# Eight filter transfers placed behind a step of the angle tables, with w_phi's transfers ahead of them

## The chip, the cores and the metric

The kernel runs on one core of one Trainium2 chip. The metric is device time in microseconds of one execution. A run's time is a little longer than the span of the profile, which goes from the first to the last profiled instruction.

The names of the engines in the profile: PE is TensorE (matmuls; PEld its weight loads), DVE is VectorE, ACT is ScalarE, POOL is GpSimd, SP is SyncE, which here only issues transfers. A "q" behind the name (SPq, POOLq) is the engine's queue of issued transfers. All transfers, whoever issues them, run on the core's 16 DMA engines.

## The reference

Eight batches, eight heads, 576 positions, head size 64. The first half is linear attention with a feature map of 2 x 128 exponentials; the second half is a gated long convolution over the sequence, done in the frequency domain with one filter per channel.

```python
def phi(x):
    proj = np.einsum('bhsd,df->bhsf', x, w_phi)
    proj = proj - np.max(np.abs(proj), axis=-1, keepdims=True)
    return np.concatenate([np.exp(proj), np.exp(-proj)], axis=-1)
q_p, k_p = (phi(q), phi(k))
kv = np.einsum('bhsf,bhsd->bhfd', k_p, v)
z = np.sum(k_p, axis=2)
num = np.einsum('bhsf,bhfd->bhsd', q_p, kv)
den = np.einsum('bhsf,bhf->bhs', q_p, z)[..., None] + 1e-06
x = (num / den)                      # heads side by side: (8, 576, 512)

proj = x @ w_proj
x1, x2, x3 = (proj[..., :D].copy(), proj[..., D:2 * D].copy(), proj[..., 2 * D:].copy())
X2 = np.fft.rfft(x2, n=S, axis=1)
H = np.fft.rfft(filter_fft, n=S, axis=0)[None, :, :]
x2_conv = np.fft.irfft(X2 * H, n=S, axis=1)
y = x1 * x2_conv * x3
return (y @ w_out).astype(np.float32)
```

The filter, 576 x 512 numbers in float32, is an input, as are w_phi (64 x 128), w_proj and w_out.

## The kernel before

The order of all work is written out by hand. PLAN (line 30) is a string of words such as `fl_load,0,1` or `Pk,0,0@4`; run (line 1043) takes them one by one and calls the method of that name with the numbers as arguments. What follows "@" is the PSUM bank. Each word issues its instructions on one engine, and each engine works through its own instructions in the order of the string. Between engines, and between engines and transfers, the waits follow from the tiles: whoever reads or overwrites a tile waits for whoever wrote or read it before.

The eight batches go through in a pipeline: for each, q and k are loaded (GpSimd issues these loads, which turn float32 into bfloat16), transposed, multiplied by w_phi (Pk, Qn, Pq), exponentiated on ScalarE (ex), reduced to their largest absolute value on VectorE (maxk, maxq), and v is scaled by GpSimd (vs). KV makes the k-v products, NE the numerators and denominators. The convolution follows (f1, f2, Ft, Fs, X2, Y1, I), then the output projection (O) and the stores (st, on SP). The first batch's q and k come in halves (loadh, line 601) and are transposed by PE (pt, line 615) and copied out (pte, line 621); later ones are transposed by transfers that SP issues (trh, line 607).

Before any of that the tables of the Fourier transform are made. VectorE and ScalarE write angles into the tile turn (ang, line 420), VectorE takes their fraction of a turn (frac, line 451, one L453 instruction for each of the four steps 3, 2, 1, 0), and ScalarE takes the sine (sin, line 457) into D, Dt and inv.

The filter enters as follows. fl_loadt (line 488) brings 64 rows into the tile flt. fl_load (line 479) brings a part of the other 512 rows into the tile fl, and is called eight times, for i of 0 to 3 and a of 0 and 1. Both are issued on SP. fz (line 485) sets one column of fl to zero on VectorE; every fl_load writes over a part of this column, so that none can be issued until fz is through.

```python
def fl_load(self, i, a):
    self.nc.sync.dma_start(
        out=self.fl[32 * i:32 * i + 32, 2 * a:2 * a + 2, :],
        in_=self.dram["filt"][288 * a:288 * a + 288].rearrange(
            "(t j) d -> t j d", j=9)[:, i:i + 6:5, :])

def fz(self, eng):
    self.eng(eng).memset(self.fl[:, :, 0:1], 0.0)
```

Once all of fl has arrived, fa (line 494) adds and subtracts its parts on GpSimd, in two instructions of 1024 columns each (L495), into a tile that shares memory with turn. PE reverses two of the results with a matrix (rev, line 504; L506), VectorE combines them (fb, line 508), and Ff (line 513) transforms them. In GpSimd's list fa is preceded by the early loads of q, k and v, and followed by a load of w_proj (w_load, line 577), by vs of the first batch and by mlo (line 738; L740), which makes the low half of q's maxima. trm (line 743; L744) transposes these on PE, and Pq (line 662; L670, L676) needs them.

w_load with "phi" issues two transfers of w_phi on SP into the tile phi, and the word w_phi (line 592) turns them into bfloat16 on VectorE. In SP's list these two stand between the third and the fourth of the eight fl_load.

Of the kernel before, what the change touches and what calls it, by code (L numbers as in the profile page):

```python
# [27 lines left out]


PLAN = """  # L30
gz,DVE sin,9 fz,DVE cz,DVE,0 loadh,q,0,0 gi_nr cz,DVE,1 gi_part gi_col cols_a cols_b cols_h
loadh,k,0,0 gi_fr ang,DVE,2 wz,23@0 wz,30@1 wz,31@0 wz,32@1 wz,33@0 ang,ACT,3 fl_loadt ident frac,3
frac,2 pt,q,0,0,0@0 pt,q,0,0,1@1 ang,DVE,1 wz,0@2 wz,34@3 wz,35@2 pt,k,0,0,0@3 ang,DVE,0
pt,k,0,0,1@2 frac,1 pte,DVE,q,0,0,1@1 zeros frac,0 fl_load,0,0 fl_load,2,1 ft,DVE fl_load,0,1
w_load,phi w_phi gi_back wz,18@1 back pte,DVE,k,0,0,0@3 Pk,0,0@4 loadh,q,0,1 sin,3 pte,ACT,q,0,0,0@0
pte,DVE,k,0,0,1@2 loadh,k,0,1 sin,2 sin,1 one Qn,0,1@0 Pk,0,1@2 pt,q,0,1,0@6 wz,27@7 sin,0 wz,14@7
fl_load,1,1 pt,k,0,1,1@7 exz ex,k,m,0,1@2 maxk,0,0@4 maxq,0,1@0 fl_load,3,1 fl_load,2,0 ex,k,p,0,0@4
pt,k,0,1,0@0 load,v,0 ex,k,m,0,0@4 pt,q,0,1,1@1 load,k,1 fl_load,3,0 maxk,0,1@2 pte,ACT,k,0,1,1@7
# [1058 lines left out]
```

## Time and profile before

| | |
|---|---|
| median of 3 runs | 293.64 us |
| lowest and highest | 292.83 and 295.11 us |
| span of the profiled execution | 291.2 us |
| granted TensorE clock, mean | 0.996 |
| HBM read, written | 33.75 MB, 9.44 MB |

The profile is of one execution, and its own time is known by its span only: 2.4 us under the median of the runs.

How to read it: the page gives the busy time of each engine and its share in 40 equal slices of some 7.3 us. A row of the timeline has the start, the length in us, the engine, the line, the operation, the tiles written and read, and in brackets how long the engine had been idle before it and what is thought to have released it. A row marked x2 or x8 is several instructions of the same kind put together, the length being that from the first start to the last end. An issue on a queue shows how long issuing took, not how long the transfer ran; the view of a tile has the time from issue to landing. The stretches give busy time of each engine in a part of the span.

### The profile page before, as it was taken

What the parts mean: (1) busy time and instruction counts of PE and PEld (TensorE: products, weight loads), DVE (VectorE), ACT (ScalarE), POOL (GpSimd) and SP (SyncE); (2) the same over time, 40 slices, a digit from 0 to 9 for tenths busy, and PEclk for the clock granted to TensorE, in tenths of its full rate; (3) what the DMA queues carried; (4) which work ended last, traced back from release to release, by engine and by line L of the source; (5) the groups of instructions that cost most, each with busy time, mean ns of one, the idle gap of its engine ahead of it and who ended that gap; (6) DMA issues with size and microseconds to landing.
All of it is one profiled execution on the core that took longest, in us unless ns stands there. A gap on an engine that the chain in (4) does not pass through costs nothing.

```text
span 291.2 us, 10275 instructions
## 1 busy us (share of the span) xinstructions
PE 274.0 (94%) x4336; PEld 194.8 (67%) x4336; DVE 252.3 (87%) x438; ACT 221.9 (76%) x367; POOL 228.5 (78%) x187
## 2 busy tenths in 40 slices
PE   6688999998999999999999999999999899999992
PEld 2346677666677866777578875776668666975851
DVE  6997898999889998998888987888999988787771
ACT  4999999987958778996897978967668988641421
POOL 8388794999968899999997999867949759955130
PEclk9999999999999999999999999999999999999998
DMA  7999999999899999998869995989604430152366
GB/s 140 230 207 175 144 204 165 139 175 181 143 192 177 163 204 159 153 119 165 122 111 156 197 169 114 163 135 191 99 14 93 84 36 2 34 108 54 69 130 184
DMA packets 72319, 40.07 MB, mean 138 GB/s; under 512 B 52496, under 2 KB 67216, under 8 KB 72272
## 3 DMA queue, kind: packets, MB, share of 16 engines
q1 hardware_dynamic: 57136, 22.62, 48.0%
q0 software_dynamic: 14816, 16.25, 36.6%
q8 instruction: 34, 0.56, 0.8%
q10 hardware_dynamic: 320, 0.52, 0.7%
q14 instruction: 13, 0.11, 0.1%
HBM read 33.75 MB, written 9.44 MB: 148 GB/s over the span
## 4 chain that ended last, share of the span: by engine, by line
PE 71%; DVE 3%; ACT 2%; issue 1%; DVEq 0%; ACTq 0%
PE ps L917 17%; PE ps L895 11%; PE ps L1016 10%; PE ps L970 8%; PE ps L773 5%; PE ps L787 4%; PE ps L876 3%; PE ps L926 2%; PE ps L670 2%; PE ps L636 2%; PE ps L643 2%; PE ps L676 2%; PE ps L869 2%; DVE mq L716 1%; PE ps L796 1%
## 5 line engine op out<-in xcount | busy, mean ns | idle before, releaser
L917 PE MATMUL ps<-xT,wproj 128*128 128x256 bf16 x512 | 64.0, 273 | 0.2 <-DMA wproj<-in_moe_w_proj_dram 0.2
L917 PEld LDWEIGHTS <-wproj 128*128 128x128 bf16 x512 | 48.1, 98 | 9.0 <-DMA wproj<-in_moe_w_proj_dram 0.4
L1005 POOL TENSOR_TENSOR yT<-cv,x1s 128x576 bf16<-128x576 f32 x31 | 39.4, 1279 | 15.6 <-ACT es L988 7.7
L716 DVE TENSOR_REDUCE mq<-ps 128x8 f32<-128x1024 f32 (+1 forms) x40 | 43.7, 1112 | 3.5 <-PE ps L643 1.5
L716 DVE TENSOR_REDUCE mk<-ps 128x8 f32<-128x1024 f32 (+1 forms) x40 | 44.1, 1112 | 2.9 <-PE ps L636 1.6
L758 POOL TENSOR_TENSOR vm<-vn,vm 128x1152 bf16<-128x1152 bf16 x16 | 34.3, 2152 | 7.4 <-ACT vm L752 7.4
L758 POOL TENSOR_TENSOR vp<-vn,vp 128x1152 bf16<-128x1152 bf16 x16 | 34.4, 2155 | 4.6 <-ACT vp L752 4.5
L698 ACT ACTIVATE Eqp<-ps 128x1024 bf16<-128x1024 f32 x32 | 32.9, 1038 | 6.1 <-PE ps L676 6.0
L854 POOL TENSOR_TENSOR SD<-xn 128x512 bf16<-128x512 bf16 x28 | 31.9, 1153 | 6.2 <-DVE xn L806 4.7
L1016 PE MATMUL ps<-wout,yT 128*128 128x512 bf16 x140 | 34.8, 379 | 0.1
L860 POOL TENSOR_TENSOR xf<-SD 128x512 bf16<-128x512 bf16 x26 | 29.7, 1155 | 6.4 <-DVE SD L854 5.9
L698 ACT ACTIVATE Ekp<-ps 128x1024 bf16<-128x1024 f32 x32 | 33.2, 1036 | 1.1 <-PE ps L636 0.7
L698 ACT ACTIVATE Eqm<-ps 128x1024 bf16<-128x1024 f32 x32 | 32.6, 1037 | 1.6 <-PE ps L676 0.8
L698 ACT ACTIVATE Ekm<-ps 128x1024 bf16<-128x1024 f32 x32 | 33.1, 1033 | 0.8 <-PE ps L636 0.7
L895 PE MATMUL ps<-wproj,XF 128*128 128x512 bf16 x128 | 31.6, 379 | 0.3 <-ACT x1s L298 0.3
L991 DVE TENSOR_TENSOR cv<-es,ps 128x288 f32<-128x288 f32 x64 | 26.3, 445 | 5.7 <-ACT es L988 4.4
L909 POOL TENSOR_TENSOR T<-T,T 128x1024 bf16<-128x1024 bf16 x14 | 29.6, 2127 | 1.7 <-DVE r L801 0.8
L970 PE MATMUL ps<-inv,T 128*128 128x288 bf16 x192 | 28.1, 286 | 0.7 <-DVE mq L716 0.4
L958 DVE TENSOR_TENSOR x1s<-ps,x1s 128x512 bf16<-128x512 f32 x32 | 21.8, 685 | 2.5 <-PE ps L917 1.1
L298 ACT COPY o<-ps 128x512 f32<-128x512 f32 x20 | 11.8, 600 | 14.4 <-PE ps L1016 12.0
L806 DVE TENSOR_TENSOR xn<-ps,r 128x512 bf16<-128x512 f32 x32 | 21.9, 689 | 0.9
L298 ACT CAST x1s<-ps 128x512 bf16<-128x512 f32 (+1 forms) x33 | 17.4, 540 | 6.7 <-PE ps L917 3.2
(184 smaller groups left out, 635.5 us busy)
## 6 DMA issues: line engine op xcount, KB each, us to landing
out_dram<-o SPq DMA_DIRECT2D x68, 128.0 KB, 2.5
vn<-in_v_dram POOLq DMA_DIRECT2D x8, 576.0 KB, 7.8
kn<-in_k_dram POOLq DMA_DIRECT2D x7, 576.0 KB, 7.8
qn<-in_q_dram POOLq DMA_DIRECT2D x7, 576.0 KB, 7.2
wproj<-in_moe_w_proj_dram POOLq DMA_DIRECT2D x3, 512.0 KB, 8.7
fl<-in_moe_filter_fft_dram SPq DMA_DIRECT2D x8, 128.0 KB, 6.0
qn<-in_q_dram POOLq DMA_DIRECT2D x2, 288.0 KB, 6.8
kn<-in_k_dram POOLq DMA_DIRECT2D x2, 288.0 KB, 8.0
```

What stands on the lines that cost most here:

```text
L298: self.nc.scalar.copy(dst, src)
L698: self.nc.scalar.activation(e, p, AF.Exp, bias=0.0, scale=1.0 if g == "p" else -1.0)
L716: self.nc.vector.tensor_reduce(out=out, in_=src, axis=AX.X, op=ALU.max, apply_absolute_value=True)
L758: self.eng(eng).tensor_tensor(out=t[:, :, :, 0:64], in0=self.at("vn", b)[:, 2 * X:2 * X + 2], in1=t[:, :, :, 64:65].to_broadcast([128, 2, ...
L854: self.eng(eng).tensor_tensor(out=o[:, :, 2 * i:2 * i + 2, :], in0=x[:, :, 0:2, :], in1=x[:, :, 2:4, :], op=ALU.subtract if i else ALU.add)
L860: self.eng(eng).tensor_tensor(out=o[:, :, 2 * i:2 * i + 2, :], in0=x[:, :, 0:4:2, :], in1=x[:, :, 1:4:2, :], op=ALU.subtract if i else ALU ...
L895: self.mm(self.pb(0), l, w[:, kt, 512:1024], start=(kt == 0), stop=(kt == 3))
L909: self.eng(eng).tensor_tensor(out=Y, in0=Y, in1=self.at(f"T{2 * e + 1}", b), op=ALU.add)
L917: self.mm(o[:, d], w[:, kt, f0 + 128 * m:f0 + 128 * m + 128], y[:, 1, ::-1, ::-1] if d else y[:, 0], start=(kt == 0), stop=(kt == 3))
L970: self.mm(self.pb(e, 0, 288), l, inv[:, 2 * e + i if i < 2 else 4 + e, :], start=(i == 0), stop=(i == 2))
L1005: self.eng(eng).tensor_tensor(out=self.at("yT", b)[:, m, 0:SEQ], in0=self.turn_of("cv", (b, m)).rearrange("p x h t -> p (x h t)"), in1=sel ...
L1016: self.mm(self.pb(0), y[:, kt, 128 * c:128 * c + 128], w[:, kt, :], start=(kt == 0), stop=(kt == 3))
```

## The change

Three words move in PLAN. fz goes from the start of VectorE's list, behind the memset gz and ahead of the column constants, to behind `frac,2`, the second of the four fraction steps. w_load,phi goes from behind the third fl_load to ahead of the first. All else keeps its order, and no instruction is added or removed.

```diff
 PLAN = """
-gz,DVE sin,9 fz,DVE cz,DVE,0 loadh,q,0,0 gi_nr cz,DVE,1 gi_part gi_col cols_a cols_b cols_h
+gz,DVE sin,9 cz,DVE,0 loadh,q,0,0 gi_nr cz,DVE,1 gi_part gi_col cols_a cols_b cols_h
 loadh,k,0,0 gi_fr ang,DVE,2 wz,23@0 wz,30@1 wz,31@0 wz,32@1 wz,33@0 ang,ACT,3 fl_loadt ident frac,3
-frac,2 pt,q,0,0,0@0 pt,q,0,0,1@1 ang,DVE,1 wz,0@2 wz,34@3 wz,35@2 pt,k,0,0,0@3 ang,DVE,0
-pt,k,0,0,1@2 frac,1 pte,DVE,q,0,0,1@1 zeros frac,0 fl_load,0,0 fl_load,2,1 ft,DVE fl_load,0,1
-w_load,phi w_phi gi_back wz,18@1 back pte,DVE,k,0,0,0@3 Pk,0,0@4 loadh,q,0,1 sin,3 pte,ACT,q,0,0,0@0
+frac,2 fz,DVE pt,q,0,0,0@0 pt,q,0,0,1@1 ang,DVE,1 wz,0@2 wz,34@3 wz,35@2 pt,k,0,0,0@3 ang,DVE,0
+pt,k,0,0,1@2 frac,1 pte,DVE,q,0,0,1@1 zeros frac,0 w_load,phi fl_load,0,0 fl_load,2,1 ft,DVE fl_load,0,1
+w_phi gi_back wz,18@1 back pte,DVE,k,0,0,0@3 Pk,0,0@4 loadh,q,0,1 sin,3 pte,ACT,q,0,0,0@0
```

## The prediction

> **What bounds the kernel now.** I read the page first, then the busy times in stretches of 10 us and of 2 us, then the timeline of the first 30 us engine by engine, and last the view of the filter tile.
>
> ```profile
> span 291.2 us, 10275 instructions
> PE 274.0 (94%) x4336; PEld 194.8 (67%) x4336; DVE 252.3 (87%) x438; ACT 221.9 (76%) x367; POOL 228.5 (78%) x187
> PE   6688999998999999999999999999999899999992
> ...
> 10.00:20.00 10.00, 7.38 (x109) 4.45 (x109) 9.55 (x20) 9.42 (x15) 6.63 (x4) 1.00 1.20 216
> 20.00:30.00 10.00, 8.59 (x173) 5.67 (x171) 8.39 (x11) 10.00 (x15) 7.54 (x5) 1.00 1.25 166
> 30.00:40.00 10.00, 9.21 (x208) 6.88 (x208) 9.02 (x14) 10.00 (x16) 9.23 (x10) 1.00 1.27 175
> 40.00:50.00 10.00, 10.00 (x117) 8.22 (x116) 9.63 (x16) 9.42 (x22) 5.90 (x6) 1.00 1.26 182
> ```
>
> The columns of a stretch are its length, then busy time of PE, PEld, DVE, ACT and POOL, the granted clock, the DMA share and GB/s. PE works 94% of the span; its loss is in the first four of the forty slices, so in the first 29 us. There VectorE (9.55 of 10 between 10 and 20 us) and ScalarE (10.00 of 10 between 20 and 40 us) are nearly full, and from 40 us on PE is. Every engine works its list in order, so a delay at 20 us is handed on to the end unless something that comes at a fixed time, such as a transfer, had been waited for later. The change lies wholly in this start. The chain of waits is of no help here: it can be followed back only to 63.87 us.
>
> Now the filter transfers and their reader:
>
> ```profile
> 0.74 0.58 SPq L489 DMA_DIRECT2D flt<-in_moe_filter_fft_dram  x1
> 1.38 1.50 SPq L480 DMA_DIRECT2D fl<-in_moe_filter_fft_dram  x3
> 2.92 1.12 SPq L582 DMA_DIRECT2D phi<-in_w_phi_dram  x2
> 4.09 2.92 SPq L480 DMA_DIRECT2D fl<-in_moe_filter_fft_dram  x5
> ...
> L480 SPq DMA_DIRECT2D fl<-in_moe_filter_fft_dram x8: 312/428/585, 1.4 to 6.7; - x8
> DMA to landing us min/median/max: 2.8/6.0/6.6
> ...
> 12.63 0.20 ACT L701 ACTIVATE ez<-zz 128x1 bf16<-128x1 bf16 x1
> 13.36 4.65 POOL L495 TENSOR_TENSOR turn<-fl 128x1024 f32<-128x1024 f32 x2 [4.53 <-ACT ez L701]
> 17.96 0.79 POOL L586 DMA_DIRECT2D wproj<-in_moe_w_proj_dram  x1
> 18.76 2.17 POOL L758 TENSOR_TENSOR vp<-vn,vp 128x1152 bf16<-128x1152 bf16 x1
> 21.93 0.25 POOL L740 TENSOR_TENSOR mh<-mq,mh 128x36 bf16<-128x36 f32 x1 [1.00 <-ACT mh L736]
> 22.14 2.15 POOL L758 TENSOR_TENSOR vm<-vn,vm 128x1152 bf16<-128x1152 bf16 x1
> ```
>
> GpSimd waits 4.53 us ahead of the two filter additions (L495). The row names ScalarE's ez, but that ended at 12.83, half a microsecond too early, and touches neither tile. The last filter transfer was issued at about 6.7, and with the longest time to landing, 6.6, it is there at 13.3: the additions wait for the last of the eight transfers. From 13.36 GpSimd then runs without a gap to 20.93 (two additions, a weight issue, one v scaling), idles 1.00 us for mh, and the maximum's low half (L740) starts at 21.93. So the filter's landing already all but decides when L740 runs; only 1.00 us lies between.
>
> **The change part by part.** *The gate.* The memset of one filter column moves from the start of VectorE's list to behind frac of step 2, and all eight transfers write over it.
>
> ```profile
> 1.09 0.06 DVE L486 MEMSET fl<- 128x4 f32 x1
> 6.33 1.28 DVE L453 TENSOR_SCALAR turn<-turn 128x864 int32<-128x864 int32 x2
> ```
>
> The first filter issue came at 1.38, soon after this memset; now it can come only after the second L453 of the pair, which ends at 7.61: at 7.66. The memset itself costs 0.06 us on VectorE in a full stretch, at most that much.
>
> *w_phi ahead.* On SP's queue its two issues (1.12 us) now go out at 1.38, behind the tail load, which has no gate. Their reader runs at 10.85 in either kernel behind VectorE's tables, so an earlier landing is worth nothing; left behind the gate they could have been late. Nothing but the filter issues waits on SP: the next thing in its list is a transpose at 21.41, and eight issues behind 7.66 are done by about 12.
>
> *When the last filter transfer lands.* Two workings, from the rows above and these:
>
> ```profile
> 2.00:4.00 2.00, 2.00 (x6) 0.76 (x5) 1.09 (x16) 0.23 (x2) 1.90 (x10) 1.00 0.84 174
> 4.00:6.00 2.00, 1.64 (x4) 0.30 (x2) 1.70 (x14) 1.54 (x3) 1.94 (x7) 1.00 1.10 229
> 6.00:8.00 2.00, 1.21 (x13) 0.87 (x14) 2.00 (x5) 1.05 (x3) 2.00 (x3) 1.00 1.11 187
> 8.00:10.00 2.00, 0.76 (x4) 0.14 (x2) 2.00 (x8) 1.93 (x5) 0.83 (x2) 1.00 1.10 244
> 10.00:12.00 2.00, 1.46 (x24) 0.97 (x26) 2.00 (x10) 1.87 (x3) 0.00 (x0) 1.00 1.16 243
> 16.00:18.00 2.00, 1.36 (x20) 0.66 (x15) 1.77 (x4) 2.00 (x4) 2.00 (x2) 1.00 1.22 209
> ...
> 8.07 0.76 POOL L596 DMA_DIRECT2D qn<-in_q_dram  x1
> DMA to landing us min/median/max: 4.3/7.3/15.8
> ```
>
> The last row is that of q's tile: GpSimd issues its last early load at 8.07, and it lands 15.8 later, at 23.9. So GpSimd's queue is full from the gate until 23.9, and the filter has to share the DMA engines with it all the way. First working, by analogy: from the first filter issue to the additions took 13.36 - 1.38 = 11.98 us; take out w_phi's 1.12 us of issuing, and 10.86 are left; 7.66 + 10.86 = 18.5. Second, by rate: the nine filter pieces and w_phi (9 x 128 KB + 64 KB, 1.24 MB) moved in the 10.5 us between 2 and about 12.5, 119 GB/s beside GpSimd's loads, which is half of the 244 of such a stretch; a transfer of 131 kB then takes 1.10 us. The first lands 2.8 after 7.66, at 10.5, seven more follow at 1.10, 18.2, and 0.3 from landing to start as before: 18.5. Both agree; the additions start 5.1 us later than now.
>
> Bounds of this term: the least is SP's pace, seven issues of 0.43 behind 7.66, landing 2.8 after the last: 13.5, start 13.8, 0.4 later than now. The most is that the filter gets through only after GpSimd's queue at 23.9: 10.8 later. I take 18.5, since it rests on the rows where both queues were loaded.
>
> *What the later start costs.* GpSimd's run of 7.57 us (13.36 to 20.93) follows unchanged; L740 then starts at 18.5 + 7.6 = 26.1 rather than 21.93, 4.1 later, the 1.00 us of idling being used up. Who waits:
>
> ```profile
> 20.03 1.98 PE L506 MATMUL ps<-turn,bk 128*128 128x512 f32 x4
> 22.23 0.23 PE L744 MATMUL ps<-ident,mh 128*128 128x128 bf16 x1 [0.21 <-POOL mh L740]
> 22.78 0.28 PE L670 MATMUL ps<-qT,wphi 64*128 64x256 bf16 x2 [0.32 <-DVE mT L300]
> 23.74 0.28 PE L670 MATMUL ps<-qT,wphi 64*128 64x256 bf16 x2 [0.34 <-ACT Ekm L698]
> 23.56 1.04 ACT L698 ACTIVATE Eqp<-ps 128x1024 bf16<-128x1024 f32 x1
> 25.26 0.43 PE L773 MATMUL ps<-vp,Ekp 64*128 64x65 bf16 x16
> ```
>
> On PE the reversal of the filter (L506) reads the second addition, which ends at 18.5 + 4.65 = 23.15 instead of 18.01; PE stands there some 3 us. Next comes the transpose of mh (L744), at 26.3; behind it queue the four q projections (L670), ScalarE's exponentials of them and the k-v product (L773), which also needs vm, GpSimd's next work after L740. All move by 4.1, less the 0.34 that the second projection waited for ScalarE, which has then long finished: 3.8 us. Does later work give it back? In 30 to 50 us PE, DVE or ACT is full in each stretch, and the only transfer that an engine waited for between 27 and 60 us is w_proj's:
>
> ```profile
> PEld L917 <- DMA wproj<-in_moe_w_proj_dram: 0.4, 1, 0.4
> ```
>
> That load is issued by GpSimd at 31.25, behind the same delayed work, so it moves along. I give back nothing.
>
> *What the early loads gain.* Half loads of q and k get the engines to themselves until 7.66.
>
> ```profile
> 10.24 0.68 PE L618 MATMUL ps<-ident,kn 128*128 128x128 bf16 x9 [1.49 <-DMA kn<-in_k_dram]
> 10.99 0.21 DVE L501 TENSOR_SCALAR bk<-idx 128x128 f32<-128x128 f32 x1
> 11.12 0.80 DVE L300 COPY kT<-ps 128x640 bf16<-128x640 bf16 x2
> 13.28 0.45 PE L618 MATMUL ps<-ident,qn 128*128 128x128 bf16 x5 [0.78 <-DMA qn<-in_q_dram]
> ```
>
> PE's 1.49 us wait for k can go, but the copy that follows stands at 11.12 right behind bk on a VectorE that is full from 6 to 12 us, so nothing reaches the end. The second halves free at most 0.78 us on PE, with VectorE and ScalarE nearly full there too. And whatever is won before 20 us ends at L506, which waits for the filter. I count it zero; at most 0.8 if the filter were in time.
>
> *The sum.* 5.1 - 1.0 - 0.3 = 3.8 us. The profiled execution spans 291.2, so 295.0; the median of the runs, 293.64, is 2.4 above that span for what lies around it. 293.64 + 3.8 = 297.4, 1.3% up. A measurement of this kernel tells about 1%, 2.9 us, from no change.
>
> **The rivals.** *The filter drains fast, and nothing is lost (not slower).* One mechanism: with the early halves gone through, the eight transfers come at a pace nearer to SP's issuing. With a pace p the additions start at 10.8 + 7p; the loss is zero up to 14.7, so p up to 0.55 us, and under 1% up to 17.6, p = 0.97. For it: the best stretches move 244 GB/s in all, and at the undivided rate 131 kB would take 0.54 us. Against it: 119 GB/s over the whole first stay, and a GpSimd queue full until 23.9. Times: 293.6 at p = 0.55, 295.3 at p = 0.8. The Trainium skill (DMA: Bandwidth & Descriptors, Anatomy of one DMA) prices a transfer on the GpSimd path at about 2 us plus its bytes over 436 GB/s; by that the 1.05 MB would be in within an estimated 4.4 us, by about 12.1, and the change would cost nothing. The trace does not agree for a busy time: a 128 KB transfer took 6.0 us to landing in the median, and only the least, 2.8, is near the rule's 2.3.
>
> *The early loads win (faster).* If the filter starts by 14.7, the second halves of q and k being earlier could take up to 0.8 us off: 292.8, still within 1%. For over 1% something behind 30 us would have to run closer, for which no row speaks.
>
> *The filter comes later still.* If GpSimd's queue gets two thirds of the engines, 80 GB/s for the filter, p = 1.64, start at 22.3: 7.6 later, 301.2. At p = 1.38 it is 299.4.
>
> *The gate does not hold the transfers.* Then 293.6. Against it: the ungated tail load went out at 0.74 and the first gated one at 1.38, behind the memset.
>
> **How the numbers follow.** The forecast with p from 0.97 to 1.35 (296.5 to 299.2): 0.53. The filter faster than that, within 1%: 0.31. Early loads winning: 0.08, of it 0.06 faster by over 1% against all rows seen. Later still: 0.06. No gate: 0.02. So faster by over 1%: 0.06; within 1%: 0.35; slower by over 1%: 0.59. The range goes from 293.4, the filter in time, to 299.4; the forecast's own is 296.5 to 299.2.
>
> **What would show it.** Right: the first filter issue near 7.7; L495 at 18.5 with GpSimd idle some 9 us ahead of it; PE idle about 3 us ahead of L506; L744 near 26.3; then the same lag, about 3.8 us, at L773 and at 60 us. Wrong: L495 before 15 us, or a lag at L744 that is gone by 60 us because some engine had room that I haven't seen; or L740 not moving since mh, not the filter, comes last.

## The result and the profile after

The changed kernel takes 304.03 us in the median of four runs (300.97 to 310.18), the kernel before 293.77 beside it. The ratio is 1.0268 with a 95% interval of 1.0213 to 1.0324, some 7.9 us; disturbed runs are left out of it, which is why it is below the ratio of the medians. The forecast was 297.4 us, the range 293.4 to 299.4: right in sign, too small by half.

The page after, and below it the stretches of the start (length, busy time of PE, PEld, DVE, ACT and POOL, granted clock, DMA share, GB/s):

```profile
span 303.9 us, 10242 instructions
PE 279.5 (92%) x4301; PEld 198.3 (65%) x4336; DVE 252.4 (83%) x438; ACT 222.3 (73%) x367; POOL 228.3 (75%) x187
PEclk9975799999999999999999979999999999999997
...
15.00:20.00 5.00, 3.89 (x38) 1.82 (x37) 4.02 (x6) 4.17 (x8) 0.00 (x0) 0.70 1.17 262
20.00:25.00 5.00, 2.02 (x26) 1.01 (x20) 3.03 (x3) 3.99 (x6) 4.58 (x2) 0.84 1.19 194
25.00:30.00 5.00, 3.52 (x21) 1.73 (x22) 1.43 (x3) 0.08 (x1) 4.99 (x5) 0.50 0.85 116
30.00:35.00 5.00, 4.78 (x107) 3.33 (x106) 2.69 (x3) 3.95 (x7) 3.99 (x3) 0.59 1.03 170
```

The busy times are those of before but for PE's, which is 5.5 us longer; that fits the slower clock. The loss is idle time, most of it in the start: GpSimd does nothing from 15 to 20 us, ScalarE works 0.08 us from 25 to 30, and the granted clock, 1.00 in these stretches before, falls to 0.50. The timeline and the view of the filter tile say why:

```profile
7.65 4.64 SPq L480 DMA_DIRECT2D fl<-in_moe_filter_fft_dram  x8
DMA to landing us min/median/max: 6.9/7.9/8.4
20.43 4.65 POOL L495 TENSOR_TENSOR turn<-fl 128x1024 f32<-128x1024 f32 x2 [11.60 <-DMA fl<-in_moe_filter_fft_dram]
22.82 1.13 PE L506 MATMUL ps<-turn,bk 128*128 128x512 f32 x2 [1.93 <-POOL turn L495]
25.12 2.07 PE L506 MATMUL ps<-turn,bk 128*128 128x512 f32 x2 [1.18 <-POOL turn L495]
27.93 0.26 POOL L740 TENSOR_TENSOR mh<-mq,mh 128x36 bf16<-128x36 f32 x1
28.24 0.29 PE L744 MATMUL ps<-ident,mh 128*128 128x128 bf16 x1 [1.04 <-POOL mh L740]
32.49 0.62 PE L773 MATMUL ps<-vp,Ekp 64*128 64x65 bf16 x16
```

The first filter issue comes at 7.65, as forecast, and the additions (L495) at 20.43, after 11.60 us of waiting that the trace itself puts down to the filter's transfers. That is 7.07 us later than before. L740 is 6.00 later, L744 6.01, the k-v product (L773) 7.23.

This execution has one more thing, which the next one lacks: a single transpose issue at 168 us takes 4.10 us, and the kernel falls back a second time there.

```profile
168.27 4.10 SPq L825 DMA_TRANSPOSE xT<-xn  x1
```

The same transpose took 1.26 us to issue before (160.56). So the size of the loss is read from the second profile below.

### The profile page after: what moved, and what is told of

Its sections match the earlier page's. It is cut to its first block, busy times and chain, and to the rows that moved or that the text cites. A ratio compares the mean times of both kernels' runs of the same rounds, so it can differ in the third digit from the quotient of the medians.

```text
span 303.9 us, 10242 instructions
## 1 busy us (share of the span) xinstructions
PE 279.5 (92%) x4301; PEld 198.3 (65%) x4336; DVE 252.4 (83%) x438; ACT 222.3 (73%) x367; POOL 228.3 (75%) x187
## 4 chain that ended last, share of the span: by engine, by line
PE 64%; DVE 3%; DMA 3%; ACT 2%; issue 2%; POOL 1%; DVEq 0%; ACTq 0%
PE ps L917 15%; PE ps L895 10%; PE ps L1016 10%; PE ps L970 6%; PE ps L773 5%; PE ps L787 3%; DMA xT<-xn 3%; PE ps L876 2%; PE ps L670 2%; PE ps L926 2%; PE ps L636 2%; PE ps L676 2%; PE ps L643 2%; PE ps L869 1%; DVE mq L716 1%
## 5 line engine op out<-in xcount | busy, mean ns | idle before, releaser
L917 PE MATMUL ps<-xT,wproj 128*128 128x256 bf16 x512 | 65.2, 276 | 2.6 <-DMA xT<-xn 2.6
L1005 POOL TENSOR_TENSOR yT<-cv,x1s 128x576 bf16<-128x576 f32 x31 | 39.3, 1277 | 15.7 <-ACT es L988 7.7
L1016 PE MATMUL ps<-wout,yT 128*128 128x512 bf16 x125 | 34.0, 380 | 0.9
L895 PE MATMUL ps<-wproj,XF 128*128 128x512 bf16 x115 | 30.6, 380 | 1.4 <-ACT x1s L298 0.4
L298 ACT CAST x1s<-ps 128x512 bf16<-128x512 f32 (+1 forms) x33 | 17.4, 541 | 9.3 <-PE ps L917 5.8
L298 ACT COPY o<-ps 128x512 f32<-128x512 f32 x20 | 11.8, 600 | 14.4 <-PE ps L1016 12.0
```

The costliest lines, as they stand in the source:

```text
L298: self.nc.scalar.copy(dst, src)
L895: self.mm(self.pb(0), l, w[:, kt, 512:1024], start=(kt == 0), stop=(kt == 3))
L917: self.mm(o[:, d], w[:, kt, f0 + 128 * m:f0 + 128 * m + 128], y[:, 1, ::-1, ::-1] if d else y[:, 0], start=(kt == 0), stop=(kt == 3))
L1005: self.eng(eng).tensor_tensor(out=self.at("yT", b)[:, m, 0:SEQ], in0=self.turn_of("cv", (b, m)).rearrange("p x h t -> p (x h t)"), in1=sel ...
L1016: self.mm(self.pb(0), y[:, kt, 128 * c:128 * c + 128], w[:, kt, :], start=(kt == 0), stop=(kt == 3))
```

## The experiments

Every experiment was timed beside the kernel before. Two tables first; the working follows. The lag is how much later than before something starts; as a mark behind the start serves GpSimd's first product of a y (L1005), at 66.07 us before.

| kernel | first filter issue | least time to landing | L495 | L740 | first L1005 | span | ratio (95% interval) |
|---|---|---|---|---|---|---|---|
| before | 1.38 | 2.8 | 13.36 | 21.93 | 66.07 | 291.2 | |
| phi_only | 2.64 | 4.1 | 14.27 | 22.39 | 66.87 | 293.6 | 1.0109 (1.0029 to 1.0189) |
| gate_3 | 4.48 | 4.7 | 16.72 | 24.57 | 68.56 | 295.0 | 1.0109 (1.0049 to 1.0170) |
| gate_5 | 5.62 | 5.8 | 18.71 | 26.22 | 70.97 | 296.8 | 1.0212 (1.0122 to 1.0302) |
| after_again | 7.65 | 6.5 | 20.04 | 27.54 | 72.08 | 297.5 | 1.0267 (1.0177 to 1.0356) |

| kernel | L495 | L740 | first L1005 | span | ratio (95% interval) |
|---|---|---|---|---|---|
| warm | 20.76 | 28.27 | 72.15 | 300.8 | 1.0271 (1.0163 to 1.0378) |
| mlo_first | 22.37 | 22.05 | 70.62 | 297.9 | 1.0185 (1.0115 to 1.0256) |
| gate_only | 21.46 | 28.98 | 72.86 | 298.1 | 1.0251 (1.0165 to 1.0337) |
| loads_behind | 19.33 | 28.31 | 74.57 | 301.0 | one run, 302.82 us |
| no_wait | 12.76 | 27.71 | 72.52 | 299.2 | 1.0212 (1.0172 to 1.0252) |
| no_filter | 12.76 | 27.70 | 71.70 | 297.2 | 1.0198 (1.0153 to 1.0243) |
| no_wait2 | 13.29 | 24.28 | 68.74 | 297.8 | 1.0048 (1.0011 to 1.0085) |
| no_filter2 | 13.11 | 24.18 | 68.17 | 294.2 | 1.0096 (1.0052 to 1.0139) |
| no_wait3 | 13.57 | 21.81 | 68.26 | 294.1 | 1.0013 (0.9967 to 1.0058) |
| no_filter3 | 13.30 | 21.81 | 65.81 | 292.2 | 0.9994 (0.9955 to 1.0033) |

(In the kernels with an added method the later lines have other numbers; the table uses those of before.)

### The changed kernel again

> The changed kernel once more. Theory A (the filter's late landing holds up GpSimd's list and with it L740, L744 and the q projections; the halved TensorE clock in PE's stalls comes on top): L495 at 20.4, L744 at 28.2, lag behind the kernel before 6.0 us at L740 and 7.7 us from 31 us on, level from there to the end; 301 to 302 us. Rival B (the lag at 166 to 176 us of the first profile, one transpose issue of 4.10 us, belongs to the change): the same step is there again, and the time is near 305.

Measured: 301.0 us (299.28 to 302.87), and in its profile

```profile
20.04 4.64 POOL L495 TENSOR_TENSOR turn<-fl 128x1024 f32<-128x1024 f32 x2 [11.22 <-DMA fl<-in_moe_filter_fft_dram]
27.54 0.25 POOL L740 TENSOR_TENSOR mh<-mq,mh 128x36 bf16<-128x36 f32 x1
30.48 0.43 PE L773 MATMUL ps<-vp,Ekp 64*128 64x65 bf16 x16
...
20.00:25.00 5.00, 2.28 (x3) 0.71 (x4) 2.21 (x2) 3.55 (x6) 4.96 (x3) 0.75 1.16 183
25.00:30.00 5.00, 3.15 (x29) 1.63 (x31) 1.88 (x3) 0.95 (x2) 4.88 (x4) 0.91 0.90 122
```

The additions are 6.68 late, L740 5.61, L773 5.22, the first L1005 6.01, and the span is 6.3 longer: all but 0.3 us of the loss is there by 66 us. There is no second step at 168 us, so rival B of the expectation falls. The clock dropped less here than in the first profile (0.75 and 0.91 against 0.84, 0.50 and 0.59), and the lag from L740 to L1005 grew by 0.4 instead of 1.5.

### The gate at other times

In this diff and the later ones each line is shortened to the words around what moves.

```diff
-frac,2 fz,DVE pt,q,0,0,0@0
+frac,2 pt,q,0,0,0@0
-gi_col cols_a cols_b cols_h
+gi_col cols_a cols_b cols_h fz,DVE
```

gate_5 is this; gate_3 has fz behind cols_a instead.

> The gate earlier, behind cols_h, so that the first filter issue comes at 5.5 instead of 7.65; w_phi still ahead. Theory A, with 12.8 us from first issue to L495 as in the changed kernel (6.9 to the first landing, then 0.8 each): L495 at 18.3, L740 at 25.9, lag 4.0 plus up to 1.5 for the clock; 297.7 to 299.3 us. The recorded working (first landing after 2.8, then 1.10 each): L495 at 16.4, lag 1.8; 295.5 us.

> The gate earlier still, behind cols_a, first filter issue near 4.4. Theory A, from issue to L495 some 12.5 to 13 us as with the two later gates: L495 at 17.1, lag at L740 2.7; 296 to 297.3 us. The recorded working (10.9 us from issue to L495): L495 at 15.3, lag 0.6 to 0.9; 294.5 us.

The first table is the answer. The earlier the gate, the smaller the lag of L740: 5.61, 4.29, 2.64 us for issues at 7.65, 5.62 and 4.48. From issue to additions it is 12.2 to 13.1 us at these three gates, not 10.9. The column of the least time to landing shows what the recorded working had wrong: that time is no constant, it rises from 2.8 to 6.9 the later the filter joins.

```profile
16.72 4.65 POOL L495 TENSOR_TENSOR turn<-fl 128x1024 f32<-128x1024 f32 x2 [7.89 <-DMA fl<-in_moe_filter_fft_dram]
24.57 0.24 POOL L740 TENSOR_TENSOR mh<-mq,mh 128x36 bf16<-128x36 f32 x1 [0.28 <-ACT mh L736]
...
18.71 4.65 POOL L495 TENSOR_TENSOR turn<-fl 128x1024 f32<-128x1024 f32 x2 [9.89 <-DMA fl<-in_moe_filter_fft_dram]
26.22 0.25 POOL L740 TENSOR_TENSOR mh<-mq,mh 128x36 bf16<-128x36 f32 x1
```

The first two rows are of gate_3, the others of gate_5. In gate_5 L740 follows GpSimd's list without a wait. In gate_3 it does not: GpSimd was through with the first v scaling at 24.28, which would have made a lag of 2.35 us, and then waited 0.28 for mh. So the 2.64 us there are not the filter's alone. The early gate has a price of its own: in gate_3 PE waited 1.51 us for the second half of k and took it up at 16.18 instead of 14.91, and the clock was 0.50 from 16 to 22 us.

### GpSimd's order

```diff
-load,q,1 fa,POOL,0
+load,q,1
-maxq,0,3@0 fa,POOL,1 em,p,0,0
+maxq,0,3@0 em,p,0,0
-ex,k,p,0,3@6 rev@4 maxk,0,2@0
-vs,POOL,p,0,0 mlo,POOL,0 vs,POOL,m,0,0
+ex,k,p,0,3@6 maxk,0,2@0
+vs,POOL,p,0,0 mlo,POOL,0 fa,POOL,0 fa,POOL,1 vs,POOL,m,0,0
-maxk,0,3@6 fb,0@4
+maxk,0,3@6 rev@4 fb,0@4
```

> The changed kernel with GpSimd's first v scaling and L740 moved ahead of the two filter additions, and the reversal on PE behind the first two q projections. Theory A: L740 and L744 are back at about 22.2, no lag there; the k-v product waits for vm, which now comes behind the additions, and lags 3.8 us; 297.5 us, up to 299 with the clock. If the lag came from the loads or the clock and not from GpSimd's order: as the change, 301.7.

```profile
22.05 0.24 POOL L740 TENSOR_TENSOR mh<-mq,mh 128x36 bf16<-128x36 f32 x1 [1.30 <-ACT mh L736]
22.37 4.65 POOL L495 TENSOR_TENSOR turn<-fl 128x1024 f32<-128x1024 f32 x2
26.98 2.15 POOL L758 TENSOR_TENSOR vm<-vn,vm 128x1152 bf16<-128x1152 bf16 x1
29.70 0.43 PE L773 MATMUL ps<-vp,Ekp 64*128 64x65 bf16 x16
```

With the filter just as late, L740 has no lag worth the name (0.12), since it no longer stands behind the additions. So L740's lag in the changed kernel comes from its place in GpSimd's list, not from the loads or the clock. The 4.44 us at L773 say less: the last filter transfer was issued at 13.0 and took at most 7.8 to landing, so it was there by 20.8, and the additions at 22.37 waited for nothing. They delay vm by their own 4.65 us, and by the order of the list they would do so with a filter in time too.

### PE kept busy in the stalls

```diff
-ex,k,p,0,3@6 rev@4 maxk,0,2@0
+ex,k,p,0,3@6 wz,40@4 ... wz,43@4 rv,0@4 wz,44@2 wz,45@2 rv,1@4 maxk,0,2@0
-ex,k,m,0,2@0 trm,0@2
+ex,k,m,0,2@0 wz,46@2 ... wz,49@2 trm,0@2
```

rv is one half of rev; each wz is two matmuls of zeros.

> The changed kernel, with zero matmuls in PE's three stalls around L506 and L744 so that PE does not idle. Theory A: L744 stays at 28.2, the granted clock stays near 1.00 from 24 to 34 us, the lag at 60 us is 6.0 to 6.3 instead of 7.7; about 300.2 us. If the halved clock costs nothing, because the stalls hide it: as the change, 301.7. If the halved clock is the main cause: under 297.

```profile
20.00:25.00 5.00, 3.58 (x13) 1.28 (x13) 2.20 (x2) 3.54 (x6) 4.24 (x2) 1.00 1.19 196
25.00:30.00 5.00, 4.10 (x36) 2.14 (x35) 1.15 (x2) 0.21 (x1) 4.99 (x5) 1.00 0.86 119
30.00:35.00 5.00, 4.73 (x137) 3.72 (x134) 3.63 (x6) 5.00 (x8) 4.47 (x3) 1.00 0.99 167
...
PE ps L920 <- DMA xT<-xn: 1.6, 1, 1.6
```

The clock stays at 1.00, and the lag does not grow behind L740: 6.34 there, 6.08 at the first L1005. That part came as expected. The time did not: the ratio is 1.0271, no better than the change. In this execution the filter landed 0.7 later than in the one above, and PE waited 1.6 us at about 84 us for a transposed x, the last row. So the clock's share of the lag is at most the 1.5 us of the first profile, and filling the stalls wins nothing that could be measured.

### The two parts alone

phi_only is the kernel before with `w_load,phi` ahead of the first fl_load; gate_only has fz moved and w_load,phi left where it was.

> The kernel before with w_phi's two transfers ahead of the filter and the gate left at the start. If the order of w_phi is worth nothing: three filter issues go out 1.2 us later, L495 at 13.4 to 14.0, within GpSimd's 1.00 us of room, L740 at 21.9; 293.3 to 293.8 us. If it carries a part of the loss: over 295.

> The gate moved, w_phi's transfers left behind the third filter issue. They are then issued at about 9.3 and land late, near 16.5; VectorE stands ahead of the w_phi cast (10.85 before) till then, and the first L636 comes at 17.5 instead of 11.65. Theory A: that lag of 6 us and the filter's of 6 us run side by side, so about the time of the changed kernel, 300 to 303 us, but with the lag there already at 17 us. If w_phi's late landing is covered: L636 at 11.7 and 301.

```profile
11.03 0.68 PE L618 MATMUL ps<-ident,kn 128*128 128x128 bf16 x9 [2.44 <-DMA kn<-in_k_dram]
11.52 0.82 DVE L300 COPY kT<-ps 128x640 bf16<-128x640 bf16 x2 [0.34 <-PE ps L618]
...
17.12 0.23 DVE L593 CAST wphi<-phi 128x128 bf16<-128x128 f32 x1 [6.21 <-DMA phi<-in_w_phi_dram]
18.16 0.61 PE L636 MATMUL ps<-wphi,kT 64*128 64x128 bf16 x8 [7.39 <-DVE kT L300]
```

The first two rows are of phi_only, the others of gate_only. Moving w_phi alone is not free, against the expectation: the first half of k is later, PE waits for it until 11.03 instead of 10.24, and the copy behind it, 11.12 before, comes at 11.52. Only 0.4 of the 0.8 us goes past the cover of VectorE's tables. L740 lags 0.46, the first L1005 0.80; the ratio is 1.0109. Moving the gate alone makes VectorE stand for 6.21 us ahead of the w_phi cast; that lag and the filter's run side by side, and the whole is as long as the change (1.0251 against 1.0267). So moving w_phi's transfers ahead takes VectorE's wait away, but once the gate has moved the time does not show it.

### What the filter shares the engines with

```diff
-pt,q,0,1,1@1 load,k,1 fl_load,3,0
+pt,q,0,1,1@1 fl_load,3,0
-load,q,1 fa,POOL,0
+fa,POOL,0
-fa,POOL,1 em,p,0,0
+fa,POOL,1 load,k,1 load,q,1 trh,k,1,0 trh,q,1,0 em,p,0,0
```

> The changed kernel with GpSimd's loads of the second batch's k and q, and the transposes that read them, moved behind the filter additions, so that GpSimd's queue is done with the first batch by about 15 us. If the filter is late because it shares the engines with that queue: the later transfers come faster than 0.8 us apart, L495 at 17.5 to 18.5. If it has its own slow pace: L495 at 20.4 as in the changed kernel. The time says little, since the second batch's loads come late; 298 us or more.

L495 came at 19.33, about 1 us sooner than in the changed kernel (20.43 and 20.04), not the 2 to 3 that were expected. The first batch's v, issued at 6.5, landed 11.5 later, at 18.0, so that GpSimd's queue was full until then even without the second batch. The expectation's "done by about 15 us" was wrong. The kernel does show the sharing: from 15 to 17 us SP's queue moved 0.43 MB and GpSimd's 0.12, where in the changed kernel it is 0.34 and 0.22, 0.56 in all in both.

### The wait taken away

Three kernels were made to let the additions read something else than the filter while its transfers stay as they are, and three more without the transfers and the gate. In the first pair the additions read zeros that GpSimd makes.

> The changed kernel, its eight filter transfers gated and sent as there, but the two filter additions read a tile of zeros made on GpSimd, so that nothing waits for the transfers; the convolution then has only the filter's 64 tail rows. Theory A (the wait of the additions is the whole loss): L495 at 11.4, L740 at 21.9, no lag at 60 us, 293.3 to 294.0 us. If sharing the engines or the clock makes up part of the loss: a lag of 1 us or more stays. If the early loads win something once nothing waits for the filter: under 292.5.

> As the last, and the eight filter transfers and the gate left out as well: no filter traffic in the start at all, the most that any place for them could free. If tables and maxima on VectorE and ScalarE bound the start: L740 at 21.7 to 21.9, 293.0 to 293.8 us. If the loads bound it: L740 before 21.4, under 292.5 us.

Both took 2% longer than the kernel before, and for a reason of their own:

```profile
12.76 4.65 POOL L499 TENSOR_TENSOR turn<-fx 128x1024 f32<-128x1024 f32 x2 [2.89 <-ACT D L467]
...
13.15 2.00 DVE L353 TENSOR_TENSOR onex<-ident 128x36 bf16<-128x36 bf16 x1
15.18 2.27 DVE L354 SCALAR_TENSOR_TENSOR one<-onex 128x18 bf16<-128x18 bf16 x1
17.37 1.21 DVE L720 TENSOR_REDUCE mk<-ps 128x8 f32<-128x1024 f32 x1
```

The additions now ran beside two tiny VectorE instructions, which took 2.00 and 2.27 us instead of 0.16 and 0.18. Each ends when one of the two additions does (15.1 and 17.4). The Trainium skill (GPSIMD Engine Reference, Specifications) says that GpSimd shares its SBUF interfaces with VectorE, with contention for VectorE instructions that have two SBUF inputs; both of these have two, and the maximum that follows, which reads PSUM, took its usual 1.21 us. The second pair reads k instead, behind a small memset that was put ahead of the last sine.

> As no_wait, but the additions read the first batch's k (as float32) and start only behind the two small VectorE instructions of one, so that they do not run beside them; the filter's place is taken by other numbers. Theory A (the wait of the additions is the whole loss): L495 at 13.5, L740 at 21.9, no lag at 60 us, 293.3 to 294.2 us. If sharing the DMA engines or the clock makes up part of the loss by itself: a lag of 1 us or more at 60 us.

> As no_wait2, and the eight filter transfers and the gate left out. If tables and maxima on VectorE and ScalarE bound the start: L495 at 12.4, L740 at 21.8 to 22.0, 293.0 to 294.0 us, so that no place for the filter could win. If the loads bound it: L740 before 21.4 and under 292.5 us.

The memset held up that sine (ScalarE's L467 at 12.26 and 12.27 instead of 10.63), so that ScalarE was 1.6 us late by 14 us and L740 2.35 and 2.25. In the third pair it stands behind the sine.

> As no_wait2, with the small memset that holds the additions back placed behind the last sine, which in no_wait2 it held up by 1.64 us. Theory A (the wait of the additions is the whole loss, apart from the clock): ScalarE has no lag at 14 us, L495 at 13.5, L740 within 0.7 of 21.9, 293.3 to 294.7 us. If sharing the DMA engines or the clock makes up a larger part by itself: a lag of 1 us or more at 60 us.

> As no_filter2, with the same mend. If tables and maxima on VectorE and ScalarE bound the start: L495 near 12.5, L740 at 21.7 to 22.6, 293.0 to 294.7 us, so that no place for the filter could win 1%. If the loads bound it: L740 before 21.4 and under 292.5 us.

```profile
13.57 4.66 POOL L500 TENSOR_TENSOR turn<-kn 128x1024 f32<-128x1024 f32 x2 [4.74 <-DMA kn<-in_k_dram]
18.18 0.79 POOL L590 DMA_DIRECT2D wproj<-in_moe_w_proj_dram  x1
21.81 0.25 POOL L744 TENSOR_TENSOR mh<-mq,mh 128x36 bf16<-128x36 f32 x1 [0.41 <-ACT mh L740]
...
20.00:25.00 5.00, 4.08 (x32) 2.02 (x33) 4.76 (x6) 5.00 (x10) 3.91 (x4) 1.00 1.22 206
25.00:30.00 5.00, 4.46 (x141) 3.68 (x142) 3.57 (x7) 5.00 (x7) 4.09 (x2) 1.00 1.59 145
...
PE ps L921 <- DMA wproj<-in_moe_w_proj_dram: 1.3, 1, 1.3
```

These rows are of no_wait3. With the gate and all eight transfers as in the changed kernel, but nobody waiting for them, L740 is at 21.81, ahead of before, the clock stays at 1.00 and the ratio is 1.0013. The lag of 1.9 us at 50 us in this profile comes later, between 35 and 44 us, where PE waits 1.3 us for w_proj (the last row): issued at 31.12, this load lands 9.8 us later, against 8.2 before and 5.7 in no_filter3. That the gated filter pushes it back is likely, but not shown. By the expectation, a lag at 60 us speaks for a cost of sharing the engines by itself; the ratio shows none, and its interval allows up to 0.6%. In after_again no engine waits for w_proj there. Without the transfers (no_filter3) the ratio is 0.9994, L740 again at 21.81.

## Why the prediction was right and wrong

**What bounds, and who waits: right.** The additions wait for the last of the eight transfers, L740 stands 7.5 us behind the additions in GpSimd's list (27.93 - 20.43, forecast 7.57), PE stood 1.93 + 1.18 = 3.1 us at L506 (forecast some 3; the match is partly luck, as the additions came 1.9 us later than forecast), and the 1.00 us of room ahead of L740 was used up to the tenth: 7.07 late at L495, 6.00 at L740. mlo_first shows that L740 is late for its place behind the additions, no_wait3 that without the wait for the filter nothing is lost that a measurement tells from zero.

**When the last filter transfer lands: wrong, and the step that failed.** It said "The first lands 2.8 after 7.66, at 10.5, seven more follow at 1.10, 18.2", and by analogy 10.86 us from issue to additions. Measured are 6.9 to the first landing, at 14.5. The last one was issued at 11.8, and with the longest time, 8.4, it is there near 20.1; so seven more come 0.80 apart, and the additions start at 20.43, 12.8 us after the issue. Both numbers were off, in opposite directions. The 2.8 was read from a transfer that went out at 1.38, before any packet of GpSimd's loads had moved; at 7.65 the engines had been busy with those loads for 4 us, and the filter's packets came in late:

```profile
8.00:10.00 2.00, 2.00 (x6) 0.71 (x5) 2.00 (x8) 1.93 (x5) 0.82 (x2) 1.00 1.09 150
10.00:12.00 2.00, 1.60 (x26) 1.00 (x26) 2.00 (x10) 1.87 (x3) 0.00 (x0) 1.00 1.11 167
...
14.00:16.00 2.00, 1.05 (x17) 0.84 (x17) 2.00 (x3) 2.00 (x4) 0.00 (x0) 1.00 1.16 273
16.00:18.00 2.00, 1.31 (x14) 0.68 (x13) 1.88 (x4) 2.00 (x5) 0.00 (x0) 0.75 1.16 278
...
q0 software_dynamic: 142, 0.15, 110.9%
...
q0 software_dynamic: 145, 0.16, 101.9%
q1 hardware_dynamic: 13, 0.03, 8.7%
...
q0 software_dynamic: 100, 0.11, 63.5%
q1 hardware_dynamic: 103, 0.17, 51.7%
```

These are 2 us stretches of the changed kernel, and below them its DMA queues (packets, MB, share of the engines' time) from 10 to 11, 11 to 12 and 15 to 16 us; q0 is GpSimd's, q1 SP's. From 7.65 to 11 us q1 moves no packet at all, though the first filter transfer has been issued; its first 13 come between 11 and 12. From 8 to 12 us the engines move 150 to 167 GB/s, nearly all of it GpSimd's loads; from 14 to 18, with the filter's transfers among them, 273 to 278. A transfer of 131 kB every 0.80 us is 164 GB/s, where 119 was assumed: once in, the filter gets more than half, with as many packets as GpSimd's queue (103 and 100) and larger ones. The Trainium skill (DMA: Bandwidth & Descriptors, Queues, rings and completion order) has each engine take turns packet by packet between its queues; that fits the second stretch, but by itself it would not leave a new queue waiting more than 3 us, as the first does. Why it waits is not shown. The gates at 4.48 and 5.62 show only that the time to the first landing grows with the time for which GpSimd's queue has run.

The rule of the Trainium skill that the prediction set against it (DMA: Bandwidth & Descriptors, Anatomy of one DMA), which is stated for the GpSimd path while the filter goes out on SP, is further from the trace than the recorded working: an estimated 4.4 us for what took about 12.5.

No rival had this step either. The filter coming later still was nearest in time, 301.2 us, but by a pace of 1.64 us; the pace measured, 0.80, was in the prediction the case for 295.3. The lateness lies ahead of the first landing, not in the pace.

**Clock: not in the sum.** The granted clock was taken as 1.00. In the changed kernel it fell to 0.50 for a while: its mean was 0.70 from 15 to 20 us, ahead of the stalls at L506, and 0.50 and 0.59 behind them. Behind L740 the lag grew by 1.5 us in one profile and 0.4 in another; in warm, with the stalls filled and the clock at 1.00, it did not grow. So the clock is the likely cause of that growth, with one or two profiles for it.

**Early loads gain nothing: right.** The first halves of q and k landed sooner, and ScalarE and VectorE ran as before until 17 us, within 0.15. no_filter3 bounds it: even without the eight transfers nothing is won that could be measured.

**w_phi ahead is worth nothing: right for the changed kernel only.** With the gate moved, the time is the same with it and without (gate_only). By itself, in front of an ungated filter, it delays the first half of k by 0.8 us.

**The sum.** 3.8 us were forecast; the second profile has 6.3, the ratio 7.9. Of the difference in the second profile, 6.68 - 5.1 = 1.6 us is the landing; the two deductions, 1.0 and 0.3, came out as 1.07 and 0.39. From L773 to the first L1005 the lag grew by 0.8, where the sum had nothing (in warm, at a clock of 1.00, by 0.1), and behind 66 us by 0.3. With 6.68 in place of 5.1 the prediction's own sum gives 5.4 us, so 299.0, where 301.0 was measured. What lies between 6.3 and 7.9 is not settled. That profile is the fastest of its four executions. In other profiles here the lag steps up by 1.3 to 4.3 us at about 84, 168 or 205 us; at 84 (warm) and 168 (mlo_first and the first profile) PE waits there 1.6 to 2.6 us for a transposed x. Whether a later start makes such waits more frequent was not tried.

## What to carry to other kernels

A transfer's time to landing belongs to the moment it was issued in: a figure from an empty machine can't be moved to a full one. Here the pace behind the first landing was better than assumed, and the wait ahead of it decided. Before holding transfers back in favour of others, look whether the others are waited for at all, and which engine's in-order list stands behind the ones that are held. A delay in such a list goes to the end unless work behind it waits for something else.

## What was not expected of the hardware

- A 131 kB transfer on SP's queue took 2.8 us to landing when issued at 1.38 us, 4.1 at 2.64, 4.7 at 4.48, 5.8 at 5.62 and, by profile, 6.1 to 7.2 at 7.65, beside the same loads of GpSimd until then. In the changed kernel SP's queue moved no packet from 7.65 to 11 us.
- Two VectorE instructions of 36 and 18 columns with two SBUF inputs took 2.00 and 2.27 us beside GpSimd additions of 2.33 us, and 0.16 and 0.18 otherwise.
- The granted clock fell to 0.50 in the changed kernel with waits of PE of 1.93 and 1.18 us at L506 and 1.04 at L744, and in gate_3, from 16 to 22 us, behind one of 1.51. It stayed at 1.00 when zero matmuls left at most 1.36 us, and in the kernel before, with one of 1.49 that ended at 10.24.
